# The same 624 steps in another written-out order, with a shorter line of loads

## The chip, the cores and the metric

The kernel runs on one core of one Trainium2 chip. That core has TensorE (PE in the profile; its weight loads are shown as PEld), VectorE (DVE), ScalarE (ACT), GpSimd (POOL) and SyncE (SP), and 16 DMA engines that serve every queue. The metric is the time of one execution in microseconds. Before the change the median of three runs is 133.91 us (133.9, 133.91 and 135.23).

## The reference

Two stages, one after the other. The first is attention inside chunks of 64 positions; the second mixes tokens with weights that are made from the tokens themselves.

```python
# q, k, v: (8 batches, 8 heads, 576 positions, 64), float32; 9 chunks of 64
scores = scale * q_c @ k_c.T                    # per batch, head, chunk: 64 x 64
scores = scores - max(scores, axis=-1)
attn = exp(scores); attn = attn / (sum(attn) + 1e-9)
x = (attn @ v_c) put together as (8, 576, 512)

wq, wk = x @ w_q, x @ w_k                       # (8, 576, 64) each
W_tok = scale * wq @ wk.T                       # (8, 576, 576)
out = relu(W_tok @ x) @ w_out                   # (8, 576, 512), float32
```

## The kernel before, in words

**Units.** The work is cut into 20 units, u0 to u19. Sixteen are whole: 256 positions (four chunks) of one batch, all heads. Four are rests: the ninth chunk of two batches together, half as much work. In the order of their numbers u2, u7, u10 and u13 are the rests. Each unit is a chain of steps. `turns` transposes q and k on TensorE (L380; L364 for a rest) and copies the result out of PSUM. `attention` computes the scores (L406 or L420), the row maximum and the subtraction on VectorE (L433, L443 or L441), the exponential on ScalarE (L453), transposes it (L465), copies it out, multiplies by v (L498; a column of ones gives the sums), and on VectorE adds 1e-9, inverts and multiplies (`den` L511, `rec` L515, `x` L525). `project` transposes x (L545), multiplies by w_q and w_k (`pj`, L555), transposes wk (L572) and lays a second copy of wq into the other half of the partitions, by a DMA on SP (L586) or by a copy. When all units of a batch are there, `mixing` forms g = wk.T x (L614), since W_tok x = wq (wk.T x); `mix_out` multiplies wq by g (L652), applies scale and relu (`rm`, L665 or L667), multiplies by w_out (L679) and copies the result to `osb` (L310), from where it is stored.

**What sets the order.** Nothing is scheduled when the kernel runs. `ORDER` (L20) is a list of words. `54P0` emits step 54 on TensorE with its PSUM output from bank 0 on; `10S` and `10V` emit step 10 on ScalarE or VectorE, for many copies may run on either. Every engine works its instructions strictly in the order in which they were emitted. Words that begin with w or n are idle products: a product of a constant tile of ones with 512 columns (w) or 128 columns (n), into a PSUM bank that nobody reads; their line is L712. All of them stand before the 43rd of the 236 TensorE steps.

**Loads.** `LOADS` (L60) is a second list: the 83 loads of q, k, v, rests and weights that GpSimd issues one after another. `q9` is q of u9, `v9a` one half of v of u9, `rq2a` a half of one part of the rests' q, `wo` is w_out. Part 2 of the rests' q and k, `rq2a rq2b rk2a rk2b`, belongs to u10 and u13 together. Before each load of a whole q or k, and only there, `pace` counts back over the loads that were issued; at the first load behind which at least `UNDER_WAY` KB (of the float32 source) were issued, GpSimd copies one element of it into `seen` (L262), and so waits until it has landed. The loads convert float32 to float16 on the way.

**Stores.** A store that comes up before the gate is open is held. The gate is a small DMA on SP that reads an element of load 82, the last one; SP issues the held stores behind it, then the others as their `osb` tiles are ready. GpSimd issues its part of the stores behind the last load. `osb` has 24 buffers.

The lines that set the length of the line of loads are these:

```python
for size, landed in reversed(sent):
    if kb >= UNDER_WAY:
        nc.gpsimd.tensor_copy(seen[:], landed())
        break
    kb += size
```

Of the kernel before, what the change touches and what calls it, by code (L numbers as in the profile page):

```python
# [21 lines left out]
n3 29P3 10V 30S w2 w2 n2 n2 33P2 11S 34V w0 n0 n0 54P0 12P1 55S 35V 56S 57S 13S w4 w4 w4 58P0 89P4  # L22
36S 59V 60V n1 n1 18P2 14P6 37P1 15V 61S 19V 16V 17V 38S w0 n0 62P0 20V 63S 21V 43P6 39P0 44V 22P5
40V 45V 41V 46V 91P2 23S 42V 90S 92S w3 w3 n3 n3 47P5 24P4 48S 93P2 25S 49P5 94V 26P4 114P0 50S 28S
27S 51P5 115S 95V 116P4 53S 117S w1 n1 n1 64P0 96S 118P2 65V 66V 67V w4 w4 97P4 119V 68P0 157P1 69S
98S 70P0 120V 52S 71S 99P6 72P0 103P4 73S 75P0 121S 104V 100V 105V 101V 106V 76S 102V w2 n2 122P2
158V 77P4 107P0 78S 83P6 108V 123S 79P1 84S 159P0 80S 85P2 160S 161P0 86V 128P4 124P6 109P3 129V
125V 130V 126V 87P2 131V 110S 127V 111P3 113S 208P4 162V 132P5 209S 81P6 133S 163V 210S 134P5 211S
74S 182P7 135S 164S 136P0 212P1 184V 185P4 138S 112S 213V 137S 165P5 186S 88V 139P0 166S 214V 183S
167P2 171P4 82S 168V 172V 169V 173V 243P1 170V 215S 187P6 140S 174V 244S 141P2 188V 216P0 142S 175P4  # L30
246P5 176S 189V 143P2 247S 217S 245V 177P3 190S 218P4 178V 153P0 147P6 219V 154S 220V 191P3 221V
148S 248P0 192V 145P4 144S 249V 193P2 146S 197P6 222P5 194V 198V 151P4 195V 199V 223S 196V 200V
224P5 152S 295P2 250V 179P3 225S 201P6 181S 296S 382P4 298S 180S 226P5 149P7 202V 251S 297V 203P0
150V 385S 299P1 204S 252P2 384V 227S 205P0 155P3 300V 207S 253S 383V 254P6 301V 156S 258P4 269P2
206S 259V 255V 302S 260V 272P1 256V 261V 270S 229P0 257V 273S 386P3 303P4 271S 262P5 387V 230S 274P6
263S 388V 231P0 304S 275V 330P2 232S 333P3 331S 305P4 276V 233P0 334S 332S 264P1 306V 307V 277S 308V
237P2 335P6 238V 235P4 234S 389S 278P0 336V 265S 309P2 279S 266P1 390P3 239P5 267V 391S 337V 310S
236S 284P0 280P2 240S 356P4 281V 285V 268S 338S 282V 359P5 283V 392P6 286V 357S 241P2 287V 360S 358V
288P0 311P1 393V 289S 361P4 394V 312V 395V 242S 313P1 290P0 314S 362V 339P3 291S 396P1 340S 292P0
420P2 294S 293S 363V 417P3 397S 421S 341P0 345P6 418S 316P2 342V 346V 343V 419S 347V 344V 446P4 317S  # L40
443P3 348V 364S 318P0 447V 422P6 319S 349P2 423V 365P4 350S 320P0 366S 424V 445S 371P4 322P1 321S
372V 425S 373V 351P0 374V 367P6 352V 444S 324P4 368V 426P0 369V 325S 370V 448P2 353P6 427S 487P7
449V 355S 354S 490P4 489S 375P0 491S 450V 326P5 376S 488S 398P4 327V 377P0 399S 323S 428P2 378V
432P6 451S 492P4 429V 433V 430V 434V 379P0 431V 328P1 381S 380S 435V 452P0 493V 400P2 436P3 401S
453S 403P2 437S 494V 556P0 404S 513P3 329S 557S 405P6 515P1 406V 514S 558P0 516S 458P2 559S 454P4
517P6 459V 495S 455V 407P1 456V 460V 457V 461V 438P0 496P4 518V 439S 411P2 497S 462P0 412S 440P4
409P5 519V 442S 441S 463S 560P2 408V 520S 502P6 464P0 561V 413P1 465S 410S 466P0 503V 521P4 504V
414S 562V 581P5 522S 583P1 467S 582S 505V 469P0 468S 584V 498P2 563S 527P4 523P6 499V 415P1 500V
501V 470S 524V 528V 506P0 525V 416S 529V 526V 585P2 507S 530V 471P6 477P0 472S 586V 531P4 564P5 228S
473P6 532V 565S 587V 478S 533P4 508P5 566P0 588S 509V 570P2 479P7 567V 568V 571V 569V 534S 589P5  # L50
474S 572V 573V 535P0 510P1 481P4 590S 480V 315S 511S 574P2 536V 482S 591P0 575S 595P6 538P3 592V
596V 512S 593V 597V 537S 598V 576P2 402S 539S 475P4 594V 577V 599P0 476S 483P2 600S 546P6 484V 540P4
547S 578P1 601P0 541V 485P2 602S 603P0 580V 548P3 605S 579V 486V 604S 606P0 549S 552P4 607V 544P1
553S 608P2 545V 614P4 609S 620P6 615V 554P0 612P1 555S 618P0 613V 621V 550P2 619S 622P0 551V 616P1
623V 542P2 617V 610P0 543V 611S
# [6 lines left out]
rk1b rq1a rk1a q6 k6 v5b v5a q8 rv1b k8 rk2b rv1a v6b v6a rk2a rq2b rq2a q9 v8b v8a k9 q11 rv2b k11  # L62
rv2a v9b k12 v11a v9a q12 q14 k14 v12a k15 v11b q15 q16 v14a v12b v15a v16a v14b k16 k17 v17a q18
v15b q17 k18 v17b v18b q19 v18a v19b v16b v19a k19
"""
GATE = 82

UNDER_WAY = 1600


class Step:
# [44 lines left out]
def kernel(  # L116
# [140 lines left out]
    def pace():  # L257

        kb = 0
# [485 lines left out]
```

## Time and profile before

| | before |
|---|---|
| median of three runs | 133.91 us |
| the profiled execution's own time | 134.89 us |
| its span in the profile | 133.1 us |
| granted TensorE clock, mean | 0.995 |
| busy: TensorE, VectorE, ScalarE, GpSimd | 119.6, 104.8, 94.0, 85.7 us |
| moved by the DMA queues | 25.56 MB; read from HBM 29.62 MB, written 9.44 MB |

The span runs from the first to the last instruction of the program; the execution around it took 1.8 us more. The profiled execution is 0.98 us longer than the median. Times inside the trace are us from the start of the span. A busy time that is a share of the span averages over stretches with different limits, so the stretches have to be read one by one: first the loads and TensorE run beside each other, from about 99 us on the stores take the place of the loads, and after 120 us only output products, their copies and their stores are left.

### The profile page before, as it was taken

What the parts mean: (1) busy time and instruction counts of PE and PEld (TensorE: products, weight loads), DVE (VectorE), ACT (ScalarE), POOL (GpSimd) and SP (SyncE); (2) the same over time, 40 slices, a digit from 0 to 9 for tenths busy, and PEclk for the clock granted to TensorE, in tenths of its full rate; (3) what the DMA queues carried; (4) which work ended last, traced back from release to release, by engine and by line L of the source; (5) the groups of instructions that cost most, each with busy time, mean ns of one, the idle gap of its engine ahead of it and who ended that gap; (6) DMA issues with size and microseconds to landing.
All of it is one profiled execution on the core that took longest, in us unless ns stands there. A gap on an engine that the chain in (4) does not pass through costs nothing.

```text
span 133.1 us, 5449 instructions
## 1 busy us (share of the span) xinstructions
PE 119.6 (90%) x2305; PEld 80.2 (60%) x2305; DVE 104.8 (79%) x197; ACT 94.0 (71%) x180; POOL 85.7 (64%) x138
## 2 busy tenths in 40 slices
PE   5986999989999999999999979999969999999920
PEld 2453667664567775868678856778647666544400
DVE  6345995987398999999999996998968998758710
ACT  3324857767469996889997997979769798655110
POOL 7995998695699847885899669799533101113300
PEclk9999999999999999999999999999999999999998
DMA  3999999999999999999999999999978899998893
GB/s 102 245 157 168 141 153 165 175 197 162 155 149 163 162 143 159 150 172 173 169 175 178 164 167 176 173 176 168 198 236 214 268 306 303 283 320 210 279 273 153
DMA packets 86907, 25.56 MB, mean 192 GB/s; under 512 B 79586, under 2 KB 82850, under 8 KB 86882
## 3 DMA queue, kind: packets, MB, share of 16 engines
q0 software_dynamic: 79504, 16.65, 143.4%
q1 hardware_dynamic: 7378, 8.56, 20.6%
q8 instruction: 18, 0.29, 0.9%
q14 instruction: 7, 0.06, 0.1%
HBM read 29.62 MB, written 9.44 MB: 293 GB/s over the span
## 4 chain that ended last, share of the span: by engine, by line
PE 54%; DMA 22%; POOL 14%; issue 4%; ACT 0%; POOLq 0%
PE ps L679 20%; PE ps L380 7%; DMA v_all<-in_v_dram 7%; DMA qkr<-in_q_dram 6%; DMA qk<-in_q_dram 6%; PE ps L545 4%; PE ps L555 4%; DMA v_rest<-in_v_dram 4%; PE ps L465 4%; POOL qk L207 4%; PE ps L498 4%; POOL v_all L215 4%; PE ps L614 3%; PE ps L652 3%; PE ps L420 3%
## 5 line engine op out<-in xcount | busy, mean ns | idle before, releaser
L679 PE MATMUL ps<-wo,rm 128*128 128x512 f16 x144 | 35.8, 380 | 1.1 <-issue 0.9
L215 POOL DMA_DIRECT2D v_all<-in_v_dram x32 | 28.3, 900 | 2.5 <-DMA qk<-in_q_dram 1.4
L433 DVE TENSOR_REDUCE mx<-ps 128x16 f32<-128x1024 f32 (+1 forms) x20 | 22.3, 1113 | 5.8 <-PE ps L406 3.3
L525 DVE TENSOR_TENSOR xs<-ps,rec 128x512 f16<-128x512 f32 x36 | 23.8, 687 | 0.4
L380 PE MATMUL ps<-ident,qk 128*64 128x128 f16 x512 | 19.3, 223 | 1.7 <-DMA qk<-in_q_dram 1.2
L453 ACT ACTIVATE es<-sh 128x1024 f16<-128x1024 f32 (+1 forms) x20 | 19.5, 976 | 1.3 <-DVE sh L443 0.7
L679 PEld LDWEIGHTS <-rm 128*128 128x128 f16 x144 | 12.5, 97 | 12.4 <-issue 0.8
L443 DVE TENSOR_TENSOR sh<-ps,mx 128x1024 f32<-128x1024 f32 x16 | 19.6, 1224 | 0.4
L310 ACT COPY osb<-ps 128x512 f32<-128x512 f32 x23 | 13.4, 590 | 8.2 <-PE ps L679 8.1
L229 POOL DMA_DIRECT2D out_dram<-osb x9 | 4.7, 527 | 21.0 <-ACT osb L310 13.9
L380 PEld LDWEIGHTS <-qk 128*64 128x64 f16 x512 | 15.6, 111 | 4.4 <-DMA qk<-in_q_dram 1.6
L207 POOL DMA_DIRECT2D qk<-in_k_dram x15 | 13.3, 888 | 3.5 <-issue 0.8
L667 ACT ACTIVATE rm<-ps 128x1024 f16<-128x1024 f32 (+1 forms) x14 | 13.4, 966 | 2.9 <-PE ps L652 2.9
L207 POOL DMA_DIRECT2D qk<-in_q_dram x15 | 13.3, 886 | 2.6 <-DMA wo<-in_moe_w_out_dram 1.0
L310 DVE COPY osb<-ps 128x512 f32<-128x512 f32 x13 | 8.9, 688 | 4.9 <-PE ps L679 4.2
L712 PE MATMUL ps<-ones 128*128 128x512 f16 (+1 forms) x45 | 10.7, 361 | 1.5 <-DVE ones L188 1.5
L310 ACT COPY xt<-ps 128x512 f32<-128x512 f32 (+1 forms) x17 | 9.2, 541 | 3.2 <-PE ps L545 2.4
L545 PE MATMUL ps<-ident,xs 128*128 128x128 f16 x144 | 11.4, 220 | 0.0
L498 PEld LDWEIGHTS <-et 64*64 64x64 f16 x576 | 7.3, 107 | 6.5 <-issue 3.3
L310 ACT COPY kt<-ps 128x512 f32<-128x512 f32 (+1 forms) x17 | 9.1, 542 | 2.5 <-PE ps L380 2.4
L555 PE MATMUL ps<-xt,wqk 128*128 128x256 f16 (+1 forms) x80 | 10.9, 262 | 0.0
L310 ACT COPY qbd<-ps 64x512 f32<-64x512 f32 (+1 forms) x18 | 9.3, 519 | 2.1 <-PE ps L364 1.5
(69 smaller groups left out, 194.6 us busy)
## 6 DMA issues: line engine op xcount, KB each, us to landing
v_all<-in_v_dram POOLq DMA_DIRECT2D x32, 128.0 KB, 6.8
out_dram<-osb SPq DMA_DIRECT2D x16, 256.0 KB, 3.6
qk<-in_k_dram POOLq DMA_DIRECT2D x15, 256.0 KB, 6.4
qk<-in_q_dram POOLq DMA_DIRECT2D x15, 256.0 KB, 6.5
out_dram<-osb SPq DMA_DIRECT2D x22, 128.0 KB, 3.5
out_dram<-osb POOLq DMA_DIRECT2D x18, 128.0 KB, 4.0
osb<-in_q_dram SPq DMA_DIRECT2D x2, 256.0 KB, 3.2
osb<-in_k_dram SPq DMA_DIRECT2D x2, 256.0 KB, 4.3
```

The source lines that it names most:

```text
L207: nc.gpsimd.dma_start(qk[u][:, t], rows_of((q, k)[t], u))
L215: nc.gpsimd.dma_start(v_home(u, i)[:, :, 0:D], of)
L310: (nc.vector.tensor_copy if eng == DVE else nc.scalar.copy)(to, of)
L380: nc.tensor.transpose(tp[half(o), j, :, r, :], of, ident[:])
L433: nc.vector.tensor_reduce(mx[:], scores(), axis=AX.X, op=ALU.max)
L443: nc.vector.tensor_tensor(out=sh[:].rearrange("p x (g r) -> p x r g", r=R), in0=in_banks(bs, 512).rearrange("p i (x r g) -> p (i x) r g", ...
L453: nc.scalar.activation(es[:].rearrange("p x s -> p (x s)"), st["sh", u][:].rearrange("p x s -> p (x s)"), AF.Exp, scale=scale_attn,)
L525: nc.vector.tensor_tensor(out=to, in0=xp()[:, :, :, 0:D], in1=by, op=ALU.mult)
L545: nc.tensor.transpose(tx[:, f, i, :], xs[u][:, i, 2 * f : 2 * f + 2, :], ident[:])
L555: nc.tensor.matmul(pj, lhsT=wqk[:, f].rearrange("p i j -> p (i j)"), rhs=st["xt", u][:, f, :], start=(f == 0), stop=(f == NF - 1),)
L667: nc.scalar.activation(to, of, AF.Relu, scale=scale_moe)
L679: nc.tensor.matmul(in_banks(bo, DM)[:, 0], lhsT=rm[:, f, i * P : i * P + P], rhs=wo[:, f, :], start=(f == 0), stop=(f == NF - 1),)
```

## The change

The change replaces `ORDER`, replaces `LOADS`, and sets `UNDER_WAY` from 1600 to 1440. No step, no load and no line of the functions is added or removed; `GATE` stays 82. Both lists hold 236 TensorE steps and 45 idle products, but of the idle products 23 have 512 columns and 22 have 128 columns, where there were 27 and 18. VectorE gets 199 steps and ScalarE 189, where each had 194: 35 steps that may run on either go from ScalarE to VectorE and 30 the other way. Many PSUM banks are numbered otherwise.

```diff
 ORDER = """
-0V 1S w0 w0 w0 w0 w0 w0 w0 n0 n0 4P0 2V 5S 3S w1 w1 w1 n1 n1 6P0 7V w1 w1 w1 8P0 31P2 9V 32S w3 n3
+0V 1S w0 w0 w0 w0 w0 w0 w0 n0 n0 4P0 2S 5V 3V w1 w1 w1 w1 n1 6P0 7S w1 w1 n1 n1 8P0 29P2 9V 30S 10V
...
 LOADS = """
-k1 q1 rq0a rq0b rk0b rk0a q3 v0b v0a v1a v1b k3 wq wk q4 k4 rv0a rv0b q5 v3b v3a wo k5 v4b v4a rq1b
+q1 rq0b k1 rq0a rk0b rk0a q3 v0b v0a wk v1b v1a k3 wq k4 q4 rv0a rv0b v3a v3b k5 q5 wo v4a v4b rq1b
...
-UNDER_WAY = 1600
+UNDER_WAY = 1440
```

What the lists make of it is seen best in the instructions as they stand on an engine, one row each with its line, its operation and what it writes and reads. Three places are shown.

The first is GpSimd's list of loads around the 43rd load. Before, from the load of k of u8 (`qk_79<-in_k_dram`) on:

```order
L207 DMA qk_79<-in_k_dram 128x8x128
L222 DMA qkr<-in_k_dram 64x16x64
L222 DMA v_rest<-in_v_dram 64x8x64
L215 DMA v_all<-in_v_dram 128x8x64 x2
L222 DMA qkr<-in_k_dram 64x16x64
L222 DMA qkr<-in_q_dram 64x16x64 x2
L262 COPY seen<-qk_79 1x1
L207 DMA qk_73<-in_q_dram 128x8x128
```

The same place of the change:

```order
L207 DMA qk_79<-in_k_dram 128x8x128
L222 DMA v_rest<-in_v_dram 64x8x64 x2
L215 DMA v_all<-in_v_dram 128x8x64
L222 DMA qkr<-in_q_dram 64x16x64
L215 DMA v_all<-in_v_dram 128x8x64
L222 DMA qkr<-in_q_dram 64x16x64
L222 DMA qkr<-in_k_dram 64x16x64 x2
L262 COPY seen<-v_rest 1x1
L207 DMA qk_73<-in_k_dram 128x8x128
```

The loads of the rests' q and k (`qkr` with 64x16x64) end at the same place of the list, position 43 of 83, and the last of them is a load of k instead of q; the 43 loads up to there are the same ones in both lists.

The second place is TensorE just ahead of the transposes of u10's rest (L364, which read `qkr`). Before, they follow the product `pj` of u7 (L555):

```order
L555 MATMUL ps<-xt_1371,wqk 128x128
L555 LDWEIGHTS wqk
L555 MATMUL ps<-xt_1371,wqk 128x128
L364 LDWEIGHTS qkr
L364 MATMUL ps<-ident,qkr 128x128
```

In the change they follow the transposes of x of u7 (L545):

```order
L545 MATMUL ps<-ident,xs_1307 128x128
L545 LDWEIGHTS xs_1307
L545 MATMUL ps<-ident,xs_1307 128x128
L364 LDWEIGHTS qkr
L364 MATMUL ps<-ident,qkr 128x128
```

So the four products of `pj` of u7 now stand behind the transposes of u10 instead of ahead of them. Nothing else of TensorE's crosses that place.

The third place is VectorE from the row maximum of u4 (`mx` with 128x16, L433) to the multiplication of u4's x (the last row). Before:

```order
L433 TENSOR_REDUCE mx_726<-ps 128x16
L443 TENSOR_TENSOR sh_756<-ps,mx_726 128x16x2x32
L511 TENSOR_SCALAR den<-ps 128x8 x2
L515 RECIPROCAL rec<-den 128x8 x2
L525 TENSOR_TENSOR xs_819<-ps,rec 128x2x256 x2
L310 COPY qt<-ps 128x512
L310 COPY xt_854<-ps 128x512
L310 COPY osb<-ps 128x512
L511 TENSOR_SCALAR den<-ps 128x8 x2
L515 RECIPROCAL rec<-den 128x8 x2
L525 TENSOR_TENSOR xs_975<-ps,rec 128x2x256 x2
```

In the change:

```order
L433 TENSOR_REDUCE mx_726<-ps 128x16
L443 TENSOR_TENSOR sh_758<-ps,mx_726 128x16x2x32
L511 TENSOR_SCALAR den<-ps 128x8 x2
L515 RECIPROCAL rec<-den 128x8 x2
L525 TENSOR_TENSOR xs_818<-ps,rec 128x2x256 x2
L310 CAST g_851<-ps 128x256
L665 TENSOR_SCALAR rm_881<-ps 128x1024
L511 TENSOR_SCALAR den<-ps 128x8 x2
L515 RECIPROCAL rec<-den 128x8 x2
L525 TENSOR_TENSOR xs_944<-ps,rec 128x2x256 x2
```

Three copies (`qt`, `xt` and `osb`, of 128x512) went to ScalarE, and two others (g of batch 0 and `rm` of u1) came from there. Ahead of the rows shown, VectorE also has one copy less (`kt` of u0) and five more (`qt` of u0, one half of `qb` of u2, `et` of u2, `wk` of u0 and `qt` of u4).

More of the change, by code (lines that the diff above doesn't have):

```diff
@@ L26 @@
[L26 to L31, printed above, removed]
@@ new lines @@
+70P5 120V 99P0 71S 72P5 159P4 73S 75P5 100V 104V 121S 101V 105V 102V 157P2 106V 122P3 158S 76V 107P6
+123S 77P0 108S 78S n2 n2 83P2 109P5 84V 110S 160S w6 79P0 85P1 128P2 86S 124P4 129V 87P6 125V 80S
+130V 126V 131V 74S 161P0 127V 88S 111P2 113S 162V 208P3 132P4 209S 81P5 133S 112V 211V 163V 210S
+134P2 212P3 135S 82S 213V 136P2 182P0 138S 137S 164S 185P1 183V 139P2 186V 184S 165P4 214V 140S
+243P0 166S 245S 171P2 167P4 172V 187P6 168V 244S 173V 169V 174V 215S 141P0 170V 246P2 142S 188V
+216P3 175P4 247S 143P0 176S 189V 217S 177P1 144S 218P2 178V 153P4 190S 147P6 219V 154V 248P0 220V
@@ new lines @@
+148S 191P4 221V 145P5 249V 192S 197P2 146S 193P6 198V 151P4 194V 199V 195V 200V 222P5 196V 152S
+295P2 382P3 250V 296S 179P4 201P6 181S 180S 223S 149P7 297V 202S 385V 251S 224P0 298V 203P1 225V
+150V 299P2 204S 226P0 252P4 384S 300V 205P1 155P5 227S 207S 253S 206V 301V 383S 254P0 156S 258P6
+255V 269P2 256V 302S 257V 272P3 271S 229P4 259V 260V 273S 261V 386P0 270S 303P1 230V 262P3 387V 304S
+274P4 263S 388V 231P6 330P1 232S 275V 333P0 331S 305P2 264P6 276V 332S 233P7 334S 306V 307V 389S
+237P4 308V 235P0 277S 238V 335P2 265S 390P1 236S 278P6 336V 391S 309P0 279S 266P4 239P1 234S 267V
@@ new lines @@
+337V 310S 280P4 284P6 240S 359P0 268S 285V 356P1 281V 286V 360S 282V 287V 392P2 358S 311P0 393V 283V
+241P6 312S 338S 357V 288P0 394V 313P1 361P4 395V 289S 339P7 242S 362V 290P0 340S 417P2 314S 291S
+420P1 363V 418S 443P0 421S 292P3 345P6 293V 294S 419S 341P4 346V 446P1 347V 342V 364S 348V 316P2
+343V 344V 422P6 317S 447S 318P2 423V 349P4 319S 396P1 365P5 397S 424V 320P2 366S 350S 398P1 321V
+444S 371P6 367P4 322P3 372V 445S 368V 373V 399V 369V 374V 425S 448P0 370V 351P2 323S 324P6 449V 352S
+375P4 325S 353P2 426P3 450V 490P5 427S 487P6 355S 354S 376V 432P2 488S 428P0 326P7 429V 433V 489S
@@ new lines @@
+434V 435V 377P4 491S 430V 328P6 451S 378V 431V 379P2 492P4 380S 327V 329S 400P0 452P1 493V 381S
+515P2 453S 558P3 401S 516S 513P0 494V 559S 403P1 514S 458P2 404S 454P6 517P4 459V 495S 455V 460V
+436P0 456V 457V 556P1 437S 461V 405P6 438P0 518V 406S 462P2 496P3 463S 519V 409P6 557S 439S 464P2
+410V 520S 440P0 560P4 465V 411P6 561V 442S 407P1 412S 521P2 497S 562V 466P6 413P7 522S 467S 408S
+441V 502P2 468V 498P4 563S 503V 469P0 499V 504V 500V 505V 581P1 414S 501V 583P6 582S 527P2 584V
+523P4 470S 415P1 315S 524V 528V 529V 525V 530V 564P0 416S 506P6 526V 565S 585P2 507S 471P0 586V
@@ new lines @@
+477P4 472S 531P6 508P7 228S 532S 587V 475P0 478S 533P1 509V 588S 570P2 566P4 571V 481P6 572V 573V
+534S 589P1 476V 535P2 510P3 473P7 590S 567V 568V 569V 511S 536S 402S 595P0 474S 591P2 596V 538P4
+597V 512S 598V 482S 574P5 592V 539V 479P0 593V 594V 540P6 575V 483P2 541S 599P1 484V 576P4 600S
+485P2 577V 537S 578P1 601P3 486V 579S 544P4 602S 603P1 546P2 604S 552P6 580S 606P1 547S 553V 545V
+542P5 607S 480S 605V 608P2 543V 620P0 614P6 609S 554P4 615S 612P2 555V 621S 550P3 613S 618P0 551S
+622P1 619V 548P2 623S 616P0 549V 610P1 617V 611S
@@ L56 @@
 """
 LOADS = """
[L61 to L64 removed]
+q1 rq0b k1 rq0a rk0b rk0a q3 v0b v0a wk v1b v1a k3 wq k4 q4 rv0a rv0b v3a v3b k5 q5 wo v4a v4b rq1b
+rk1b rk1a rq1a q6 k6 q8 v5b v5a k8 rv1b rv1a v6a rq2b v6b rq2a rk2b rk2a k9 v8a q9 v8b k11 rv2b q11
@@ L65 @@
+rv2a v9b q12 k12 v9a v11b q14 v11a k14 q15 k15 q16 v12a v12b q17 k16 v14b k18 v14a q18 v18a k17 v15a
+v15b v16a v19a v17b k19 v19b v16b q19 v17a v18b
 """
 GATE = 82
-UNDER_WAY = 1600
+UNDER_WAY = 1440
 class Step:
```

32 lines of the change are left out of this document (4 added, 28 removed).

## The prediction

> **What bounds the kernel now.** I read the page's head and slices first, then the busy times by stretch, then the chain that ended last.
>
> ```profile
> span 133.1 us, 5449 instructions
> ...
> PE 119.6 (90%) x2305; PEld 80.2 (60%) x2305; DVE 104.8 (79%) x197; ACT 94.0 (71%) x180; POOL 85.7 (64%) x138
> ...
> PE   5986999989999999999999979999969999999920
> ...
> DVE  6345995987398999999999996998968998758710
> ...
> PEclk9999999999999999999999999999999999999998
> ...
> GB/s 102 245 157 168 141 153 165 175 197 162 155 149 163 162 143 159 150 172 173 169 175 178 164 167 176 173 176 168 198 236 214 268 306 303 283 320 210 279 273 153
> ```
>
> TensorE is busy almost without a hole from about 13 us to 127 us, but a busy TensorE doesn't say what paces it: idle products and early waits are in that. The last row is the other half: from 10 to 95 us the DMA engines deliver a nearly flat 140 to 180 GB/s, whatever TensorE does. The same by stretch (columns: length, then busy us and instructions of PE, PEld, DVE, ACT and POOL, then granted clock, DMA share and GB/s):
>
> ```profile
> 13.50:36.00 22.50, 20.81 (x481) 14.02 (x480) 16.76 (x32) 15.65 (x31) 18.22 (x29) 1.00 1.91 164
> 36.00:52.80 16.80, 16.36 (x306) 11.13 (x299) 16.12 (x33) 13.60 (x27) 13.76 (x22) 1.00 2.33 156
> 52.80:98.90 46.10, 43.98 (x971) 33.00 (x972) 41.84 (x78) 40.50 (x81) 36.35 (x58) 1.00 1.97 178
> 98.90:120.20 21.30, 21.23 (x376) 13.61 (x374) 18.12 (x41) 16.78 (x33) 3.83 (x8) 1.00 0.89 274
> 120.20:127.20 7.00, 7.00 (x33) 2.91 (x32) 5.28 (x8) 1.90 (x3) 2.11 (x4) 1.00 0.87 250
> ```
>
> Three things are close to full at once. Up to 52.8 us it is the loads, with VectorE beside them from 36 us on (16.12 of 16.80); after that TensorE (43.98 of 46.10, then 21.23 of 21.30), with VectorE and ScalarE at about nine tenths. The chain says where the one gives way to the other (start, length, what):
>
> ```profile
> 44.04 8.63 DMA qkr<-in_q_dram
> 52.66 0.14 issue
> 52.80 0.61 PE ps L364 x8
> ...
> 79.19 0.85 issue
> ...
> 97.01 1.26 issue
> ...
> 120.20 7.03 PE ps L679 x32
> ...
> 127.25 0.58 ACT osb L310
> ```
>
> The end hangs on a load: the rests' q for u10 and u13 lands at 52.66, and from 52.80 on TensorE works, with two stops, until 127.2. So **the end = landing of that load + what TensorE still has to do + a tail of 5.9 us** (copy, store, end of program; 133.1 - 127.2). Between 52.80 and 127.22 lie 74.4 us, of which the two stops are 2.1.
>
> **The change, part by part.**
>
> *The landing.* The 43 loads up to and with the last rests' loads are the same ones in both lists, 13,056 KB of source (512 KB for a whole q or k, 256 for a half of v, 128 or 256 for a piece of a rest, 1024 for w_out, 128 for w_q or w_k). The engines deliver at a flat rate, so the last of them lands when as much has been moved as before: 52.7 us. Only the order inside those 43 differs. The whole list is 27,904 KB in both, so the last load, and with it the gate, should stay where they are:
>
> ```profile
> 98.89 0.69 SPq L234 DMA_DIRECT2D gate<-qk  x1
> ```
>
> *The shorter line.* 1440 instead of 1600 KB holds GpSimd a little longer ahead of each q or k. It costs nothing as long as the engines have work when it lets go.
>
> ```profile
> qk<-in_q_dram POOLq DMA_DIRECT2D x15, 256.0 KB, 6.5
> ...
> POOL seen L262 <- DMA v_all<-in_v_dram: 2.3, 3, 1.4
> ```
>
> A q load lands 6.5 us after its issue. 1440 KB of source is 720 KB of float16, and at 164 GB/s that is 4.4 us of work still queued when the wait ends; 1600 KB is 4.9. An issue takes GpSimd about 0.9 us. No row shows how short the line may be before the rate drops. The bounds: nothing, or the difference of 0.5 us at each wait that finds the engines dry, and the 6.5 us say that most of a load's time is queueing, so I take nothing. A single dry wait ahead of u10 moves the end by 0.5.
>
> *Idle products.* Four of 512 columns become four of 128.
>
> ```profile
> 1.46 3.38 PE L712 MATMUL ps<-ones 128*128 128x512 f16 x9 [1.46 <-DVE ones L188]
> ...
> 14.41 0.81 PE L712 MATMUL ps<-ones 128*128 128x512 f16 x3
> ```
>
> Three wide ones take 0.81 from first start to last end, so at most 0.27 each; four of them are at most 1.1 us and, since the narrow ones cost something too, about 0.6. All stand ahead of the load that decides, so TensorE only waits longer for it: 0.
>
> By the Trainium skill ("TensorE: Matmul & The Clock Gate", section "What's actually happening") the clock is gated to half unless the array has been busy through a window of about 3.4 us, which speaks against fewer idle products. The trace agrees with its start: the first nine (seven wide, two narrow) took 3.38 us, while three wide ones at 14 us took 0.81. No run here shows a second drop, and the granted clock is 1.00 in every stretch above, so the sum by the rule is the same unless the change opens such a window.
>
> *TensorE's order around the deciding load.* `pj` of u7 now stands behind u10's transposes.
>
> ```profile
> 52.19 0.39 PE L555 MATMUL ps<-xt,wqk 128*128 128x128 f16 x4
> ```
>
> This adds 0.2 (pitch alone, as the products overlap their neighbours) to 0.4 us to what is left after the landing. I take **+0.4**, since the wait in front of the transposes hid the whole group before. Everything else of TensorE's changes places on one side of that point, with the same instructions: 0 in the sum.
>
> *VectorE.* The copies that change engine ahead of u4's `den` cost, by form:
>
> ```profile
> L665 DVE TENSOR_SCALAR rm<-ps 128x1024 f16<-128x1024 f32 x4 | 4.9, 1219 | 0.3 <-PE ps L652 0.3
> ...
> L310 DVE COPY kt<-ps 128x512 f32<-128x512 f32 x3 | 2.1, 685 | 1.4 <-PE ps L380 1.4
> ...
> L310 DVE COPY qbd<-ps 64x256 f32<-64x256 f32 x3 | 1.3, 421 | 0.1
> ...
> L310 DVE CAST wk<-ps 128x128 f16<-128x128 f32 x3 | 0.9, 285 | 0.0
> ...
> L310 DVE COPY qt<-ps 128x512 f32<-128x512 f32 x1 | 0.7, 680 | 0.0
> ...
> L310 DVE CAST g<-ps 128x256 f16<-128x256 f32 x1 | 0.4, 425 | 0.7 <-PE ps L614 0.7
> ```
>
> Added: two `qt` at 0.68, half a `qb` at 0.42, `et` of a rest (not in the trace on VectorE; as many columns as that half, and at most a full 0.68; I take 0.42), `wk` 0.285, g 0.425, `rm` 1.22: 4.13. Removed: `kt`, `qt`, `xt` and `osb`, all 128x512, at 0.685: 2.74. So **+1.4 us** of VectorE's queue ahead of u4's `den`. What covers it are VectorE's own waits there (in brackets: idle time before the instruction):
>
> ```profile
> 22.57 1.23 DVE L433 TENSOR_REDUCE mx<-ps 128x16 f32<-128x1024 f32 x1 [1.62 <-ACT wt L310]
> ...
> 35.01 0.69 DVE L310 COPY osb<-ps 128x512 f32<-128x512 f32 x1 [2.38 <-PE ps L679]
> ...
> 36.05 0.33 DVE L511 TENSOR_SCALAR den<-ps 128x8 f32<-128x8 f32 x2 [0.35 <-PE ps L498]
> ...
> 52.85 1.22 DVE L443 TENSOR_TENSOR sh<-ps,mx 128x1024 f32<-128x1024 f32 x1
> ```
>
> 4.35 us of idle time against 1.4, and the largest wait (2.38, for an output product) goes with the copy that waited. The `den` at 36.05 itself follows the load of u4's v, which has the same bytes ahead of it as before. From there to u8's subtraction at 52.85, VectorE has 19.15 us of work by form before and 19.16 after (34 and 35 instructions, summed in the same way). So 0, and if the cover fails, VectorE passes on up to 1.4 us, because from 36 us on it has no slack to make it up. Summed over the whole kernel VectorE loses 1.1 us (two `rm` at 1.22 and some 128x512 copies fewer, more small ones) and ScalarE gains 0.6; ScalarE has 5.6 us free of the 46.1 in its fullest stretch.
>
> *The tail.* SP issues its last four stores in one piece to 129.3, close behind the last copies; the last word of both orders is the same copy on ScalarE and its single store.
>
> ```profile
> 126.38 2.90 SPq L229 DMA_DIRECT2D out_dram<-osb  x4
> ```
>
> I leave the tail at 5.9.
>
> *The sum.* 52.8 + 74.4 + 0.4 = 127.6 for TensorE's end, 133.5 of span, and with 1.8 us around it 135.3 for a profiled execution. The profiled execution of before took 134.89, the median is 133.91; the same 0.98 off gives **134.3 us**, 0.3% above before. A difference under 1% is about what a measurement of this kernel can't tell from no change.
>
> **The rivals.**
>
> *VectorE doesn't swallow its 1.4 us.* The five additions ahead of u4's row maximum sit between subtractions and the `den` of u2 and u3, so x of u2, then g of batch 0 and `rm` of u1 come later in one chain. If `den` of u4 starts after 36.05 by more than a few tenths, the subtraction of u8, its exponential and TensorE's transposes of it slide by as much, and so does all that follows. For it: VectorE is full from 36 us on. Against it: the 4.35 us of waits. Full price 134.3 + 1.4 = 135.7, and up to 137.0 if the lost time makes TensorE arrive late at later steps too, for most copies in both lists are due just when TensorE wants them. Slower by 1.3 to 2.3%. Chance 0.30.
>
> *The two stops don't come again.* TensorE stood still for 0.85 and 1.26 us with nothing to wait for in the profile, once inside a run of 32 products. Nothing in `ORDER` makes them, so another order need not have them. Then TensorE ends at 125.5 and the time is 134.3 - 2.1 = 132.2. Against it: the profiled execution is 0.98 longer than the median, so the usual run may already lack one of them, and the gain then stays under 1%. Chance of over 1%: 0.16.
>
> *The line runs dry*, or the clock drops once. At 0.5 us a time, four dry waits ahead of 52.7 us give 134.3 + 2.0 = 136.3; against it speaks the flat rate. A drop of the clock for a stretch like the first one would cost what the first nine products lost: 3.38 less 7 x 0.27 less a little, about 1.4 us, so 135.7. Chance 0.07 together.
>
> *The change does less than it says.* Loads come in multiples of 128 KB, so the wait falls on whole loads and 1440 acts like 1536, 1600 like 1664 or 1792; and fewer wide idle products only lengthen a wait. Then nothing but +0.4 is left, which is the forecast.
>
> **How the numbers follow.** The forecast, 134.3, has 0.47, and with small waits of up to 0.9 us either way it stays within 1%. The slower cases have 0.30 + 0.07, of which about 0.01 stays within 1%; the faster case has 0.16, and a hundredth or two more for small waits that go. So faster 0.18, same 0.46, slower 0.36. The range goes from 132.2, the price of the stops, to 137.0, the dearer end of the first rival; what lies outside is half of the fast case and the worst of the slow ones, about 2 in 10.
>
> **What would show it.** Right: the last rests' load lands at 52 to 53 us and the gate at about 99; TensorE runs from there for 72 to 75 us; u4's `den` starts at about 36 and the first `mx` wait of VectorE after it is short. Wrong: DMA GB/s below 140 in the slices up to 95 us (the line), `den` of u4 after 37 (VectorE), a stretch of idle products at twice the pace (the clock), or TensorE's holes after 53 us adding to more than 3 us, which would mean that the order itself, not a pinned load, decides.

## The result, and the profile after

On one chip, 20 runs of each kernel: the change takes 135.72 us in the median (134.3 to 137.77), the kernel before 134.94 us (133.41 to 136.56). The ratio is **1.0105, 95% interval 1.0075 to 1.0136**: about 1% slower. Every ratio here and below compares only those runs of a kernel that lie within 1.5% of its fastest, while the medians are over all its runs, so that the quotient of two medians comes out another way (1.0058 here). The forecast was 134.3 us, 0.3% above the 133.91 us that the kernel before had taken then; in this comparison it took 134.94. The range (132.2 to 137.0) holds the time, but the case that I held likeliest, "within 1%", was just missed, and the sum behind it was wrong in two terms that nearly cancelled.

| | before | after |
|---|---|---|
| the profiled execution's own time, us | 134.89 | 136.59 |
| span, us | 133.1 | 134.8 |
| busy: TensorE, VectorE, ScalarE, GpSimd, us | 119.6, 104.8, 94.0, 85.7 | 119.8, 102.9, 96.4, 85.9 |
| u10's transposes start, us | 52.80 | 50.51 |
| gate opens, us | 98.89 | 99.83 |
| TensorE ends, us | 127.22 | 126.34 |
| from there to the end, us | 5.9 | 8.5 |

The profiled execution of the change is 0.9 us longer than its median; a second one (the first experiment) took 134.43 us, and there the gate opened at 98.71 us, TensorE ended at 125.55 and the tail from there was 7.1 us.

The page of the change: its span, TensorE's busy time, TensorE in 40 slices of 3.37 us, and what the DMA engines moved in each slice.

```profile
span 134.8 us, 5439 instructions
...
PE 119.8 (89%) x2305; PEld 80.2 (60%) x2305; DVE 102.9 (76%) x202; ACT 96.4 (71%) x175; POOL 85.9 (64%) x138
...
PE   5999899899998999978999998988999999999400
...
GB/s 108 248 162 164 160 176 161 186 195 156 142 160 169 152 150 135 172 163 171 119 171 171 167 159 166 170 159 166 138 287 250 271 252 306 249 309 255 275 258 157
```

TensorE does the same work and is through earlier, yet the program ends later. Between 17 and 98 us three slices lie under 140 GB/s (135, 119 and 138); before there was none. The same stretches as before (length, busy us and instructions of PE, PEld, DVE, ACT, POOL, clock, DMA share, GB/s):

```profile
36.00:52.80 16.80, 16.05 (x304) 11.18 (x302) 15.47 (x31) 14.17 (x27) 13.65 (x21) 1.00 2.22 152
52.80:98.90 46.10, 43.17 (x944) 31.92 (x943) 41.56 (x79) 41.09 (x76) 35.23 (x56) 1.00 1.94 163
98.90:120.20 21.30, 21.30 (x382) 13.33 (x381) 17.07 (x41) 16.76 (x33) 5.05 (x10) 1.00 0.91 271
120.20:127.20 7.00, 6.14 (x29) 2.56 (x27) 2.77 (x4) 3.37 (x6) 1.59 (x3) 1.00 0.91 282
```

From 52.8 to 98.9 us it is 163 GB/s where it was 178. The chain that ended last says the same in its own way (start, length, what):

```profile
54.11 7.81 DMA v_rest<-in_v_dram
...
75.56 6.13 DMA v_all<-in_v_dram
...
84.00 7.33 DMA v_all<-in_v_dram
...
119.32 2.71 PE ps L679 x12
122.06 0.59 ACT osb L310
122.82 3.58 DMA out_dram<-osb
```

Before, no load stood in the chain after 52.66 us. Now there are three, each of them issued shortly behind a copy of GpSimd into `seen`; and the chain ends with a store that has to land before ScalarE gets its `osb` buffer back. I read GpSimd's waits for the line (us in total, times, longest) as the cause, which the experiments put to the test, and TensorE's (in brackets: idle time, and what ended it) as the effect:

```profile
POOL seen L262 <- DMA v_all<-in_v_dram: 7.6, 8, 2.0
```

```profile
60.33 1.08 PE L380 MATMUL ps<-ident,qk 128*64 128x128 f16 x32 [0.80 <-DMA qk<-in_q_dram]
...
61.96 0.44 PE L498 MATMUL ps<-v_rest,et 64*64 64x65 f16 x16 [0.55 <-DMA v_rest<-in_v_dram]
...
84.17 0.45 PE L498 MATMUL ps<-v_all,et 64*64 64x65 f16 x32 [0.57 <-DMA v_all<-in_v_dram]
```

The largest group of `seen` waits was 2.3 us in 3 waits before; now it is 7.6 in 8, and all of them together went from 6.4 us in 8 waits to 12.2 in 13. What the late stores do shows on SP's queue, from the gate to the last store:

```profile
99.83 0.69 SPq L234 DMA_DIRECT2D gate<-v_all  x1
100.58 15.97 SPq L237 DMA_DIRECT2D out_dram<-osb  x19
116.65 14.55 SPq L229 DMA_DIRECT2D out_dram<-osb  x19
```

38 stores in 30.6 us with hardly a pause among them (0.08 us from one to the next, once 0.5). The last is issued 3.6 us after the last copy is there (ScalarE's last copy ends at 126.96). In the kernel before it was the same with less of it:

```profile
99.64 13.72 SPq L237 DMA_DIRECT2D out_dram<-osb  x17
113.46 15.82 SPq L229 DMA_DIRECT2D out_dram<-osb  x21
```

29.6 us, again with no gap over 0.5 us, and the last store is issued 1.0 us behind the last copy. So SP's queue can bound the end beside TensorE, in the kernel before too, and a later gate can then move the end. The runs with an early gate below test that.

### The profile page after: what moved, and what is told of

Its sections match the earlier page's. It is cut to its first block, busy times and chain, and to the rows that moved or that the text cites. A ratio compares the mean times of both kernels' runs of the same rounds, so it can differ in the third digit from the quotient of the medians.

```text
span 134.8 us, 5439 instructions
## 1 busy us (share of the span) xinstructions
PE 119.8 (89%) x2305; PEld 80.2 (60%) x2305; DVE 102.9 (76%) x202; ACT 96.4 (71%) x175; POOL 85.9 (64%) x138
## 4 chain that ended last, share of the span: by engine, by line
PE 54%; DMA 18%; DVE 9%; ACT 5%; POOL 4%; issue 3%; SPq 0%; DVEq 0%; POOLq 0%; ACTq 0%
PE ps L679 16%; DMA v_all<-in_v_dram 10%; PE ps L380 7%; DMA v_rest<-in_v_dram 6%; PE ps L712 6%; PE ps L498 4%; PE ps L555 4%; PE ps L465 4%; PE ps L545 4%; DVE mx L433 3%; POOL qk L207 3%; PE ps L614 3%; PE ps L652 3%; DMA out_dram<-osb 3%; PE ps L406 2%
## 5 line engine op out<-in xcount | busy, mean ns | idle before, releaser
L433 DVE TENSOR_REDUCE mx<-ps 128x16 f32<-128x1024 f32 (+1 forms) x20 | 22.2, 1111 | 3.8 <-PE ps L406 3.6
L310 ACT COPY osb<-ps 128x512 f32<-128x512 f32 x24 | 14.1, 591 | 7.5 <-PE ps L679 5.4
L667 ACT ACTIVATE rm<-ps 128x1024 f16<-128x1024 f32 (+1 forms) x15 | 14.8, 998 | 2.2 <-PE ps L652 2.0
L229 POOL DMA_DIRECT2D out_dram<-osb x8 | 4.2, 529 | 18.6 <-DVE osb L310 6.0
L310 ACT COPY qbd<-ps 64x512 f32<-64x512 f32 (+1 forms) x20 | 10.3, 517 | 2.4 <-PE ps L364 1.0
L310 DVE COPY osb<-ps 128x512 f32<-128x512 f32 x12 | 8.3, 688 | 4.9 <-DMA out_dram<-osb 2.9
L310 ACT COPY et<-ps 128x512 f32<-128x512 f32 (+1 forms) x19 | 10.4, 552 | 2.2 <-PE ps L465 1.8
L310 ACT COPY xt<-ps 128x512 f32<-128x512 f32 (+1 forms) x18 | 9.7, 540 | 3.3 <-PE ps L545 3.1
L545 PE MATMUL ps<-ident,xs 128*128 128x128 f16 x144 | 11.2, 220 | 0.0
L555 PE MATMUL ps<-xt,wqk 128*128 128x256 f16 (+1 forms) x80 | 11.0, 262 | 0.0
```

What stands on the lines that cost most here:

```text
L310: (nc.vector.tensor_copy if eng == DVE else nc.scalar.copy)(to, of)
L433: nc.vector.tensor_reduce(mx[:], scores(), axis=AX.X, op=ALU.max)
L545: nc.tensor.transpose(tx[:, f, i, :], xs[u][:, i, 2 * f : 2 * f + 2, :], ident[:])
L555: nc.tensor.matmul(pj, lhsT=wqk[:, f].rearrange("p i j -> p (i j)"), rhs=st["xt", u][:, f, :], start=(f == 0), stop=(f == NF - 1),)
```

## The experiments

Each ratio is against the kernel before, measured on the same chip in the same comparison. "Lists" means `ORDER` and `LOADS` together.

**The change again, and each of its two parts alone.** Three kernels: the change unchanged; the lists of before with the short line; the lists of the change with the long line. The edits of the latter two:

```diff
 # lists of before
-UNDER_WAY = 1600
+UNDER_WAY = 1440
```

```diff
 # lists of the change
-UNDER_WAY = 1440
+UNDER_WAY = 1600
```

The change again:

> The changed kernel once more, for a second profile. Theory G (the gate): the end is set by the stores, which start when the last load lands (99.8 us in the first profile against 98.9) and then take SP about 31 us to issue; the span is then the gate + 35 us, and TensorE ends no later than before (126 to 127 us). Theory O (the order): the instructions' order makes TensorE late, and it ends after 128 us. Ratio to before by both: 1.010.

The short line alone:

> Before, with 1440 KB in line and nothing else changed. If the shorter line is what opens the gate late (theory G, cause L1: the DMA engines run dry behind the waits), the gate opens 0.5 to 1.5 us later than in before and the ratio is 1.005 to 1.010, with slices of DMA that fall under 140 GB/s. If the order of steps or of loads is the cause, the ratio is 1.000 within 0.003.

The lists alone:

> The change with 1600 KB in line, its own orders kept. Cause L1 (the shorter line): back to 1.000 to 1.004, gate at about 98.9. Otherwise (order of steps, or order of loads): still 1.010.

Measured (before: 134.72 us):

| | 1600 KB in line | 1440 KB in line |
|---|---|---|
| lists of before | 1 | 135.54 us, 1.0121 (1.0043 to 1.0199) |
| lists of the change | 133.49 us, 0.9919 (0.9861 to 0.9977) | 135.59 us, 1.0105 (1.0004 to 1.0206) |

The line is what costs: 1.2% on the old lists (1.0061 by the medians) and 1.0105/0.9919 = 1.9% on the new ones, a figure that the two intervals leave uncertain by about a point. The lists by themselves gain 0.8%, which I hadn't expected. The stretch from 52.8 to 96 us by kernel: before, the change, the short line alone, the lists alone (last number: GB/s).

```profile
52.80:96.00 43.20, 42.35 (x917) 32.02 (x918) 40.09 (x76) 38.47 (x78) 35.45 (x56) 1.00 2.03 171
```

```profile
52.80:96.00 43.20, 40.27 (x888) 30.06 (x887) 38.70 (x76) 38.33 (x72) 33.05 (x52) 1.00 1.94 160
```

```profile
52.80:96.00 43.20, 41.66 (x898) 30.83 (x895) 39.87 (x75) 37.91 (x76) 34.36 (x54) 1.00 1.96 163
```

```profile
52.80:96.00 43.20, 41.55 (x929) 30.88 (x926) 40.88 (x79) 40.30 (x74) 33.72 (x53) 1.00 2.02 178
```

171 and 178 with 1600 KB, 160 and 163 with 1440, whichever lists. The other profiled executions of this study agree: 161 to 164 with 1440 KB, 169 to 179 with 1600. With the lists alone the gate opens at 96.48 us, 3.4 and 2.2 us earlier than in the two profiles of the change. From 29 us on the chain of that kernel holds no load at all; it is nearly all TensorE's work, with stops of 0.46 us at 77.96, 0.33 at 83.41 and 1.00 at 95.14:

```profile
93.03 0.86 PE ps L679 x4
95.14 1.00 issue
96.14 1.04 PE ps L679 x4
```

One expectation missed. With the short line alone the gate opened no later than in the profiled execution of before (98.89 us), which by itself was 0.98 us longer than the median:

```profile
98.97 0.69 SPq L234 DMA_DIRECT2D gate<-qk  x1
```

So a late gate is not shown by that pair. Over all fourteen profiled executions the last load lands at 98.2 to 99.8 us with 1440 KB in line, at 95.9 to 98.9 with 1600 and at 95.5 and 96.2 with 2000.

**The change's steps with the loads of before**, at 1600 KB. The edit puts the `LOADS` of before under the `ORDER` of the change:

```diff
 LOADS = """
-q1 rq0b k1 rq0a rk0b rk0a q3 v0b v0a wk v1b v1a k3 wq k4 q4 rv0a rv0b v3a v3b k5 q5 wo v4a v4b rq1b
+k1 q1 rq0a rq0b rk0b rk0a q3 v0b v0a v1a v1b k3 wq wk q4 k4 rv0a rv0b q5 v3b v3a wo k5 v4b v4a rq1b
...
-UNDER_WAY = 1440
+UNDER_WAY = 1600
```

> The order of steps of the change alone, with the list of loads and the 1600 KB of before. Theory O: 1.010 remains, since the order of steps is what costs. Theory G, whichever of the two parts of the loads makes the gate late: 1.000 to 1.003, gate at about 98.9; some waits of TensorE for single loads may add up to 0.5 us, because the loads are not in the order in which this list of steps asks for them.

Measured: 137.29 us, 1.0266 (1.0188 to 1.0344), more than either theory had. The lists belong together. The old list brings k of u5 behind w_out, while the new steps ask for it first; TensorE stands for 1.76 us, and a stretch of lower clock follows (the mean granted clock of 28 to 40 us is the third number from the end):

```profile
31.16 1.06 PE L380 MATMUL ps<-ident,qk 128*64 128x128 f16 x16 [1.76 <-DMA qk<-in_k_dram]
```

```profile
28.00:40.00 12.00, 9.99 (x142) 6.59 (x145) 4.84 (x10) 5.30 (x11) 9.93 (x17) 0.72 2.04 165
```

**A longer line than either.** If 160 KB less cost that much, more might gain. 2000 KB under both pairs of lists:

```diff
-UNDER_WAY = 1440    # lists of before: 1600
+UNDER_WAY = 2000
```

On the lists of the change:

> The change with 2000 KB in line instead of 1440. Theory L (the line runs too short at 1440 KB: GpSimd is let go so late that the engines have less queued than they can work on, and every load behind that lands later; the longer line of 1600 took 2.1 us off the change, the last load landing 2.2 us earlier): more in line goes on helping until the engines always have enough; with 1440 to 1600 worth 1.9%, 2000 should be 0.98 to 0.993 of the kernel before, and the last load should land at 94 to 96.5. Rival T (1600 is already enough, what is left is TensorE's work and the stores): the same as with 1600, 0.99 to 0.995, the last load at 96 to 97. Rival W (a longer line lets loads that are not urgent compete with those that are, and GpSimd's issues stall): slower than with 1600, above 0.995.

On the lists of before:

> The kernel before with 2000 KB in line instead of 1600. Theory L: 1600 to 1440 cost 1.2% there, so 2000 gives a further gain of 0.5 to 1.5%: 0.985 to 0.995, the last load landing at 95 to 97.5 instead of 98.9. Rival T: 0.997 to 1.003. Rival W: above 1.003.

Measured (before: 134.16 us): 137.49 us, 1.0235 (1.0155 to 1.0316), and 136.0 us, 1.0159 (1.0094 to 1.0224). Both are slower, so the first theory missed. The ratios lie where rival W put them, but its mechanism isn't it: the loads were not held up. With the lists of the change the rate stayed at 178 GB/s and the last load landed at 95.5 us, earlier than in any other kernel. That didn't help the gate, which opened at 100.53 us, and at 99.65 with the lists of before, where the last load landed at 96.2: SP works in order, and ahead of the gate stands its copy of wq (`wt`, L586), which needs TensorE's products and began at 99.98 and 99.09 us. A load of q took 7.3 us from issue to landing with 2000 KB in line and 5.9 us in the change, from these two pages:

```profile
qk<-in_q_dram POOLq DMA_DIRECT2D x15, 256.0 KB, 7.3
```

```profile
qk<-in_q_dram POOLq DMA_DIRECT2D x15, 256.0 KB, 5.9
```

What came late was TensorE, without waiting for a load. Its stops in the kernel with 2000 KB and the new lists (two of five; `issue` in the brackets means that the profile knows nothing that ended them):

```profile
74.46 0.36 PE L380 MATMUL ps<-ident,qk 128*64 128x128 f16 x6 [0.79 <-issue]
...
87.59 0.21 PE L498 MATMUL ps<-v_all,et 64*64 64x65 f16 x1 [1.70 <-issue]
```

They are of the same kind as the two stops that the prediction had found in the kernel before:

```profile
80.05 0.59 PE L679 MATMUL ps<-wo,rm 128*128 128x512 f16 x2 [0.85 <-issue]
...
98.28 0.19 PE L406 MATMUL ps<-kt,qt 64*64 64x64 f16 x1 [1.26 <-issue]
```

The profile has no name for what ends them, but two things in the trace do. First, with TensorE's instructions (4610 products and weight loads, and 21 of its sequencer that wait or drain) numbered in order of time, the stops fall one or two behind 704, 960, 2240, 2752, 3008, 3264, 3776 and 4032, all of the form 704 + 256 k, in kernels with quite different orders. Second, there is a DMA queue that the profile calls one of instructions; in the page of before:

```profile
q8 instruction: 18, 0.29, 0.9%
```

18 packets of 16,384 bytes, which at 4631 instructions is about 256 instructions each. TensorE's stops end at nearly the same time after such a packet (between: from the packet's end to the end of the stop):

```
kernel                 stop ends   packet ended   between (us)
before                   80.05        78.67          1.38
before                   98.28        96.95          1.33
lists before, 2000       62.89        61.51          1.38
lists before, 2000       82.58        81.15          1.43
lists change, 2000       74.46        73.14          1.32
lists change, 2000       87.59        86.04          1.55
```

In the fourteen profiled executions of this study there are 26 unnamed stops of a product of 0.4 us and more. Every one ends 1.2 to 1.65 us after a packet of that queue, one or two instructions behind such a number. So these are **waits for the next block of TensorE's own instructions**. By the Trainium skill ("Runtime: NRT & Kernel Launch", section "Instruction fetch mechanics") an engine's instructions are refilled in blocks of 16 KiB, 256 instructions, over a DMA queue that the sequencer drives, and crossing a boundary is "mostly hidden". The trace agrees on the block and on the queue; but here it was the less hidden the longer the line (the executions profiled in this study, by the length of the line; stops of 0.4 us and more):

```
in line   kernels   stops in each        sum of stops, mean (us)
1440 KB      6      0, 0, 1, 1, 1, 1          0.6
1600 KB      6      1, 2, 2, 2, 3, 3          2.3
2000 KB      2      4, 5                      4.3
```

The packets begin the later the more loads are queued: if a block is asked for when TensorE passes the boundary one block earlier (which the trace doesn't show, so this is assumed), the median wait of a packet between 20 and 92 us is 2.43 to 3.05 us with 1440 KB in line, 2.85 to 3.33 with 1600, and 4.13 and 4.25 with 2000. TensorE's waits for loads behind 52.8 us go the other way: 1.1 to 2.9 us in sum in each of the six executions with 1440 KB, 0.2 at most in the other eight. So the length of the line has two prices, and they run against each other: too short, and loads land late; too long, and TensorE's instructions do. That the blocks are what makes 2000 KB slower is read from these stops; no run changes the blocks and leaves the line as it is.

**The gate three loads earlier.** SP's gate reads load 79 instead of the last one, 82; nothing else changes. The same edit on the change and on the kernel before:

```diff
+GATE_ON = 79
...
+        if n_load == GATE_ON:
+            gate_on = last
         if n_load == GATE:
-            graph.queue.append((lambda last=last: open_gate(last()), lambda: moved))
+            graph.queue.append((lambda last=gate_on: open_gate(last()), lambda: moved))
```

On the change:

> The change with the gate opened by the landing of load 79 instead of load 82; everything else as in the change, the line at 1440 KB. Load 79 landed 2.6 to 3.2 us ahead of load 82. Theory G (behind the gate 38 stores of SP stand in a queue that needs 29 to 31 us, so the end is the gate plus 34 to 36 us, and a late load costs time through the gate rather than through TensorE): the end comes 1 to 2.6 us earlier than the change's, which was 1.0105 of before: 0.985 to 1.003. Rival T (TensorE's work sets the end, the stores only follow): 1.005 to 1.015, no change. Rival C (stores beside the last three loads slow these, q of u19 lands after 100 us and TensorE waits for it): 1.015 to 1.03.

On the kernel before:

> The kernel before with the gate opened by the landing of load 79 (one half of v of u19), which landed 4.0 us ahead of load 82 there; the line stays at 1600 KB. Theory G: 0.975 to 0.992. Rival T: 0.995 to 1.005. Rival C (k of u19, the last load, lands after 101 us, beside the stores, and TensorE waits for it): 1.005 to 1.02.

Measured: on the change 134.07 us, 1.0013 (0.9972 to 1.0054), against 1.0105; on before 134.51 us, 0.9961 (0.9907 to 1.0015). On the change the early gate gives back nine tenths of a per cent, nearly the whole loss against the kernel before, with the line as short as it was. The gate opened at 95.21 us, 4.6 and 3.5 us earlier than in the two profiles of the change, and SP again worked through its stores with no gap over 0.5 us:

```profile
95.97 16.77 SPq L238 DMA_DIRECT2D out_dram<-osb  x19
112.83 14.86 SPq L230 DMA_DIRECT2D out_dram<-osb  x19
```

The tail stayed at 7.1 us; what came earlier was TensorE's end, at 124.6 us against 126.3 and 125.6. On before the effect can't be told from none, and the edit did less there than it says: load 79 had landed at 93.80 us, but SP's copy of wq ahead of the gate began only at 96.78, so the gate opened at 97.34, 1.6 us earlier and not 4. In that execution TensorE had three block stops (2.2, 0.7 and 1.0 us), ended at 127.9 us, and SP did have pauses (one of 1.4 us and two of 1.0); there TensorE was the bound.

**Is it SP?** Two edits on the best kernel so far (new lists, 1600 KB): the early gate as above, or the whole-tile stores that come up after the gate moved from SP to GpSimd:

```diff
-                    store(out[b, 2 * P * m : 2 * P * m + P, :], osb[:])
+                    store(out[b, 2 * P * m : 2 * P * m + P, :], osb[:], QUEUES[1 if "open" in st else 0])
```

The stores moved:

> The change's orders with 1600 KB in line (133.49 us, 0.992 of the kernel before), and the seven whole-tile stores that come up after the gate is open issued by GpSimd in place of SP; SP keeps 31 of its 38. Theory G (from the gate on SP issues one store after another without a pause, 38 of them in 31 us, and this queue ends after TensorE has): SP is relieved of 7 x 0.75 = 5 us and the end falls back to TensorE's end plus 5.4 us, which was seen where SP did have pauses: 125.4 + 5.4 = 130.8 against a span of 132.3, so 0.975 to 0.987 of the kernel before. Rival B (the stores are bound by the bytes that the DMA engines can write, not by SP): no change, 0.989 to 0.996. Rival P (GpSimd's queue, with its own waits for copies, holds stores that stand behind slower ones): 0.996 to 1.01.

The early gate:

> The change's orders with 1600 KB in line and the gate on the landing of load 79 in place of load 82, 3.9 us earlier there. Theory G: SP begins its 38 stores up to 3 us earlier and the end is again bounded by TensorE's end plus 5.4 us: 0.975 to 0.988 of the kernel before, TensorE no earlier. Rival B (bytes): stores and the last three loads share the engines, the sum of bytes is the same, 0.988 to 0.996. Rival C (the last loads land late and TensorE waits): 0.996 to 1.01.

Measured (before: 134.65 us): 134.07 us, 0.9953 (0.9905 to 1.0002), and 133.93 us, 0.9955 (0.9901 to 1.0009). Neither gains on 0.9919; I had expected 0.975 to 0.988, and both lie where rival B, the bytes, had put them. With the stores moved, the gaps between SP's stores add to 6.7 us instead of 3.1, and the tail behind TensorE is 5.5 us instead of 6.9. But TensorE itself ended later, at 126.5 us instead of 125.4, with block stops of 1.4 and 0.5 us. The early gate was not early at all in its profiled execution: load 79 had landed at 94.81 us, but the gate opened 1.0 us later than without the edit (96.48), because the copy of wq stood ahead of it:

```profile
96.90 0.46 SPq L589 DMA_DIRECT2D wt<-wt  x1
97.45 0.69 SPq L235 DMA_DIRECT2D gate<-v_all  x1
```

TensorE ended at 128.1 us there, with stops of 0.6, 1.4 and 1.3 us. So with 1600 KB TensorE was the bound in these executions, and whether SP's issues or the bytes bound the stores behind the gate isn't settled: one issue of SP's takes 0.3 to 2.1 us, and what makes the long ones long isn't shown.

Both edits together on the change with its 1440 KB, where the blocks had nearly all come in time:

> The change with its 1440 KB in line, the gate on the landing of load 79, and the seven late whole-tile stores issued by GpSimd. With 1440 KB the instruction blocks of TensorE arrive in time, and with the early gate alone (1.0013 of the kernel before, span 131.7, TensorE's end 124.6) SP still had no pause between its 38 stores and ended 2.5 us after the last copy. Theory G: with seven stores fewer SP has pauses, the tail falls from 7.1 to about 5.4 us, and the time to 0.985 to 0.995 of the kernel before. Rival B (the engines write no faster, bytes bound the end): 0.997 to 1.006, as with the early gate alone. Rival P (GpSimd's stores stand behind one another's copies, and land last): 1.0 to 1.01, with SP pausing and the last store being one of GpSimd's.

Measured (before: 134.18 us): 134.67 us, 1.0018 (0.9974 to 1.0062), no better than the early gate alone. The gaps between SP's stores add to 6.0 us and the last store to land is one of GpSimd's, the sign that rival P had named; rival B's range holds the time as well. TensorE ended at 127.5 us instead of 124.6, and one of its rows shows a part of that:

```profile
103.69 0.38 PE L682 MATMUL ps<-wo,rm 128*128 128x512 f16 x1 [1.27 <-issue]
```

A block again, this time among the stores. It is one stop in one execution; that the stores on GpSimd's queue bring such stops about isn't shown.

**The idle products.** Four narrow idle products of the change made wide again, so that there are 27 and 18 as before:

```diff
-... 6P0 7S w1 w1 n1 n1 8P0 ... w3 w3 w3 n3 n3 31P2 ... w6 n6 n6 14P2 ... w4 w4 n4 37P4
+... 6P0 7S w1 w1 w1 n1 8P0 ... w3 w3 w3 w3 n3 31P2 ... w6 w6 n6 14P2 ... w4 w4 w4 37P4
```

> The change (1440 KB) with four narrow idle products made wide again, so that there are 27 of 512 and 18 of 128 columns as before; all else as in the change. The prediction's term of 0 (TensorE only waits longer for the loads): 1.005 to 1.015, as the change itself. Rival (the narrow ones let the chain up to u4 start earlier, the 0.6 us is real): 1.012 to 1.02. Rival (the clock is granted more often with wide ones, which a drop in one stretch of some runs would fit): 0.995 to 1.005.

Measured (before: 134.65 us): 135.8 us, 1.015 (1.0058 to 1.0242). The interval holds the change's own ratio, so no effect is shown, in either direction.

## Why the prediction was right and wrong

*"The shorter line ... I take nothing"*: **this step failed.** It costs about 1.2% (1.6 us) on the old lists and 1.9% (2.5 us) on the new. I argued that 6.5 us from issue to landing must be mostly queueing. With 1440 KB it is 5.9 us in the change, and the rate falls as well; with 2000 it is 7.3, and on the lists of the change the rate doesn't rise over the 178 GB/s of 1600 (on those of before it goes from 171 to 177). Had 1600 KB been more than the engines need, only the time from issue to landing would have fallen. My bound, 0.5 us for each dry wait, was the right kind, and the rival "the line runs dry" gave 136.3 for four of them; I gave it 0.07 together with the clock because the rate looked flat, but a flat rate can be set by the line just as well as by the engines. Nor was it as flat as I read it: between 10 and 93 us the slices of before go from 141 to 197 GB/s. The sign I had named did come: slices of 135, 119 and 138 GB/s. With this step fell another, *"the last load, and with it the gate, should stay where they are"*: the gate opens at 99.83 and 98.71 us in the change, and at 96.48 with the same lists and 1600 KB.

*"52.8 + 74.4 + 0.4"*: **this failed too.** I held the landing of the rests at 52.7 us to be pinned by the bytes ahead of it, and everything after it to follow. But with the same bytes ahead of it the last of these loads landed at 49.7 to 52.4 us in the other thirteen profiled executions: the one that I had was the latest. In the early-gate variant of before, with the same loads in the same order, it landed at 50.70, and TensorE began the transposes of u10 only at 53.31, without a wait:

```profile
53.31 0.39 PE L367 MATMUL ps<-ident,qkr 128*128 128x128 f16 x4
```

In the change they began at 50.51, 2.3 us before my fixed point, and the last load landed at 50.87, when TensorE was already at them:

```profile
50.51 1.21 PE L364 MATMUL ps<-ident,qkr 128*128 128x128 f16 x14
```

The load ended a wait of 0.2 us in the one execution I had; it didn't set the pace. So the lists were free to gain, and they did, 0.8%, where I had put +0.3%. I had no term for that: "Everything else ... 0 in the sum". In the four profiled executions with the old lists those transposes start at 51.4 to 53.3 us, in the nine with the new ones at 50.5 to 52.4; of the four with old lists the earliest is the one with 1440 KB. Which of the many moved steps brings that wasn't taken apart. In the change the sum reads 50.5 + 75.8 + 8.5: the middle term is 1.0 us over my 74.8, for the two stops of 2.1 us are gone and waits for loads of 2.9 us have come.

*VectorE's +1.4 us, hidden*: **right**, and the rival that gave it 0.30 fell. `den` of u4 starts at 33.85, not late but 2.2 us earlier than before, and after a wait, so the added copies were covered:

```profile
33.85 0.40 DVE L511 TENSOR_SCALAR den<-ps 128x8 f32<-128x8 f32 x2 [1.70 <-PE ps L498]
```

Summed over the kernel my reckoning of the copies was off: VectorE is busy 1.9 us less and ScalarE 2.4 us more, where I had 1.1 and 0.6.

*The tail "left at 5.9"*: **failed.** I read "SP issues its last four stores in one piece ... close behind the last copies" as a matter of the last four. They looked like one piece because the rows that I had asked for began there; they were the end of a queue that had hardly paused since 99.64. In the change the tail is 8.5 us and takes more than TensorE's earlier end gave. It holds beyond that one execution: where SP kept its 38 stores the tail is 7.0 to 8.5 us with 1440 KB in line (five executions) and 4.9 to 6.9 with 1600 and 2000 (seven).

*The rival of the two stops*: its event came in part. They are absent from the profiled execution of the change, and TensorE did end earlier; its second profile has one, of 0.93 us. But by the table above they are fewer because the line is shorter, the same cause that made the loads late, and the longer tail took the gain. "Nothing in ORDER makes them" was right: where they fall is set by the count of instructions, how long they are by the DMA queue.

*Idle products 0*: not contradicted. *"The change does less than it says"*: fell; the step from 1600 to 1440 is felt.

That the range held the time is luck: it is due to two opposite errors, -0.8% for the lists and +1.9% for the line, against +0.3% and 0. Of those 1.9% the early gate gives back 0.9. Where the rest goes stays open: TensorE's waits for q and v (2.9 us in the change) speak for late loads, but the block stops that went weigh about as much, single executions scatter by as much as is to be explained, and with the new lists TensorE ends no later in the five executions with 1440 KB (124.6 to 127.5 us) than in the three with 1600 (125.4 to 128.1).

The best kernel found is the lists of the change with the line of before: 133.49 us, 0.9919 of the kernel before (0.9861 to 0.9977), faster than both.

## What to carry to other kernels

A limit on transfers in flight can have a price on both sides: vary it up and down before taking it for free, above all when the transfer rate looks flat, since the limit itself may be what makes it so. When an engine stops for a reason that the profile doesn't name, number its instructions: stops at a constant distance (256 here) point to the blocks in which its own instructions arrive, which may queue with your loads. And look past the end of the busiest engine: a queue that issues without a pause into the tail is a second bound, and what it waits for at its start can belong to the critical path. Look there at what stands ahead in the same queue, too: a gate opens no sooner than the instruction before it is done.

## What the runs showed of the hardware that I had not expected

TensorE's instructions arrive in packets of 16,384 bytes, on a DMA queue that the page counts as a share of the same 16 engines as the data's; a block that came late cost up to 2.2 us, and work went on 1.2 to 1.65 us after its packet had ended.

A stop can cost twice. In the kernel with 2000 KB and the new lists the stop of 1.70 us, up to 87.59 us, was followed by a lower granted clock (third number from the end):

```profile
85.50:92.00 6.50, 4.80 (x61) 2.52 (x60) 3.35 (x9) 2.85 (x5) 4.87 (x8) 0.74 2.18 168
```

A mean of 0.74 over 6.5 us is 1.7 us of full clock lost, or 3.4 us at half. The prediction cited the Trainium skill ("TensorE: Matmul & The Clock Gate", section "What's actually happening") on a gate with a window of about 3.4 us, and said that no run showed a second drop; this one and the one with the mixed lists do. But the stop alone doesn't decide it: the early-gate variant of before had a stop of 2.19 us at 21.6 us and kept its clock, which is 1.00 from 20 to 32 us there.
